# Keeping w_in's tiles as high and low parts between three passes of PackIn

## The chip, the core and the metric

The kernel runs on one core of a Trainium2 chip. The metric is the device time of one execution in microseconds (us). The engines are named as the profile does: PE (TensorE; PEld is its weight load), DVE (VectorE), ACT (ScalarE), POOL (GpSimd) and SP (SyncE, which here only issues DMA transfers).

## What is computed

Attention in two steps over 32 packed rows, then two feed-forward blocks, all in float32:

```
p_packed = softmax(p k^T / 8) v            8 batches, 8 heads, 32 x 576 x 64
x = softmax(q p_packed^T / 8) p_packed     as 4608 x 512
h = x @ w_in                               512 x 2048
x = (h * sigmoid(h)) @ w_out               2048 x 512
out = (((x @ w1) * (x @ w2)) @ w3) @ wo2
```

## The kernel before

**High and low parts.** A float32 product is made of three matmuls in the type fp32r: `mm3` (lines 97 to 100) multiplies high by high, low by high and high by low part. A part pair is made by `split_hi` (L82, a cast, on ACT as an activation or on DVE as L86) and `split_lo` (L91, a subtraction, on DVE or on POOL).

**The first half of the program** (to about 860 us) is a list of 256 items `(b, f, m)`: batch, half of its 576 rows, block of 128 of the 2048 hidden columns. For an item, `emit_h` makes ps_h (six matmuls), `emit_g` the activation: sg on ACT (L841), gg on DVE (L846), its high part gh on ACT and its low part gl on POOL; `emit_x2` multiplies by w_out three items later (`LAG = 3`) into four PSUM banks ps_x. At the end of each half the banks are emptied into xs, two of them by DVE (L883). ps_h has two buffers, so it waits for the gg of two items before.

**Where h's left factor comes from.** Attention output is never formed for the product with w_in: `PackIn` multiplies the packed rows by w_in instead (m = p_packed w_in, for two batches at once) and stores m in the DRAM tensors m_d; `fetch` loads blocks of it (tile mr), splits them (mq: high part on DVE, low part on POOL) and uses them as weights of ps_h. `Pack` and `Spread` are the two attention steps; their work (sbd, mbd, x, s, e, pk) runs mostly on DVE and ACT.

**PackIn** runs three times, for batches 2 and 3, 4 and 5, 6 and 7; its due times (`pack_in`) are items 44 to 66, 102 to 126 and 166 to 190. Each pass goes through the 16 tiles of w_in (128 x 512). The source tiles lie in the DRAM tensor wi_d, stored at the program's start. `load_w` loads one into wz (tag z, NZ = 6 buffers), and splits it into the pair wi (WI = 3 buffers): the high part on ACT (128 x 512), the low part on POOL. `steps` loads three tiles ahead; then for each tile:

```
ps = bank("ps_m")
mm3(ps[0:64 * n], m3[0], m3[1], w[:, 0], w[:, 1], True, True)
self.load_w(i + WI)
ms = at.tile([128, 512], F32, tag="ms", name="ms", bufs=NM)
split_hi(ms[0:64 * n], ps[0:64 * n], False)
```

and two `move`s store ms, whose tag has NM = 2 buffers, to m_d. The tag wi also holds raw (source words of w_in and w_out at the start) and sums (of `decode_late`).

**What sets the order.** Three streams are advanced by due times (`due`): x (attention), y (PackIn) and z (`decode_late`, late weights). `move` issues on SP's queue. `store` puts a transfer off: `flush`, called once per item, issues it on ACT's queue, with age 1 at the second flush. The framework then places each instruction by its own model of time, and keeps one in-order queue for each engine. All 16 DMA engines serve SP's queue and ACT's.

Of the kernel before, what the change touches and what calls it, by code (L numbers as in the profile page):

```python
# [9 lines left out]
F32 = mybir.dt.float32  # L10
F32R = mybir.dt.float32r
# [12 lines left out]
def attention_swiglu_chain(  # L24
# [36 lines left out]
    CD = DM // 128  # L61
# [15 lines left out]
    NSLOT, LAG, WI, KQ, NZ, NM = 8, 3, 3, 2, 6, 2  # L77
# [3 lines left out]
    def act_copy(dst, src, mul=1.0):  # L81
        return A.activation(out=dst, in_=src, func=ACTF.Copy, scale=mul)  # L82

    def split_hi(hi, src, on_vector=False):
        if on_vector:
            V.tensor_copy(out=hi, in_=src)  # L86
        else:
            act_copy(hi, src)

    def split_lo(lo, src, hi, eng=None):  # L90
        (eng or V).tensor_tensor(out=lo, in0=src, in1=hi.bitcast(F32), op=ALU.subtract)  # L91
# [5 lines left out]
    def mm3(dst, wh, wl, xh, xl, start, stop):  # L97
        T.matmul(out=dst, lhsT=wh, rhs=xh, start=start, stop=False)  # L98
        T.matmul(out=dst, lhsT=wl, rhs=xh, start=False, stop=False)  # L99
        return T.matmul(out=dst, lhsT=wh, rhs=xl, start=False, stop=stop)  # L100
# [10 lines left out]
    def move(out, in_, eng=DMA):  # L111

        out, in_ = (x.bitcast(F32) if x.dtype == F32R else x for x in (out, in_))
        with tc.issue_after(behind[eng]) if eng in behind else ExitStack():
            return eng.dma_start(out=out, in_=in_)
# [3 lines left out]
    def store(out, in_, age=1):  # L119

        stores.append([age, out, in_])
# [14 lines left out]
    dram = ctx.enter_context(tc.tile_pool(name="dram", bufs=1, space=bass.MemoryType.DRAM))  # L136
    const = ctx.enter_context(tc.tile_pool(name="const", bufs=1))
    ident = const.tile([128, 128], F32, name="ident")

    wi_d = dram.tile([4, DM, 512], F32, name="wi_d")  # L140
    w12_d = dram.tile([128, KM2 // 2, 2, 7, 2, 2, 128], F32, name="w12_d")
    w34_d = [dram.tile([128, 512], F32, name=f"w34_d{i}") for i in range(KM2)]
    late_d = {n: dram.tile([128, 512], F32, name=f"late_d{n}") for n in range(KM2, MID)}
# [5 lines left out]
    at = attn.enter_context(tc.tile_pool(name="at", bufs=1, side="right"))  # L149
# [13 lines left out]
    def bank(name):  # L163
        return ps_f.tile([128, 512], F32, tag="f", name=name)


    class Decode:
# [7 lines left out]
        def __init__(self, raw, z, ps=None):  # L175
            def word(dtype, t):
                return raw.bitcast(dtype).rearrange("p (n t) -> p n t", t=2)[:, :, t]

            high = word(F32, 1) if ps is None else ps
            act_copy(high, word(F32, 1), 2.0**-112)  # L180
            act_copy(word(I32, 0), word(U32, 0), 2.0**-29)
            high = high.bitcast(I32)
            V.tensor_scalar(out=z, in0=high, scalar1=3, scalar2=None, op0=ALU.logical_shift_left)

            V.scalar_tensor_tensor(
                out=word(I32, 0), in0=high, scalar=-(2**31), in1=word(I32, 0),
                op0=ALU.bitwise_and, op1=ALU.bitwise_or,
            )
            G.tensor_tensor(out=z, in0=z, in1=word(I32, 0), op=ALU.add)
            self.z = z.bitcast(F32)  # L190
# [41 lines left out]
    def m_blocks(plain):  # L232
        return blocks("mbd", [128, 2, CD, 2, 2, 32], plain)
# [263 lines left out]
    class PackIn:  # L497
# [2 lines left out]
        N = 17  # L500
        HOOKS = {}

        def __init__(self, bs):
            self.bs = bs
            self.w = {}

        def load(self):
# [2 lines left out]
        turn0 = turn1 = prepare = load_v = split_v0 = tail = load  # L510

        def load_w(self, i):
            if i < 4 * CD:
                g, c = divmod(i, CD)
                z = at.tile([128, 512], F32, tag="z", name="wz", bufs=NZ)
                move(out=z, in_=wi_d[g, 128 * c:128 * c + 128])
                t = at.tile([128, 2, 512], F32R, tag="wi", name="wi", bufs=WI)
                split_hi(t[:, 0], z)
                split_lo(t[:, 1], z, t[:, 0], G)
                self.w[i] = t  # L520

        def steps(self):
            n = len(self.bs)
            for i in range(WI):
                self.load_w(i)
            yield
            mbd_use[0] = self
            for i in range(4 * CD):
                g, c = divmod(i, CD)
                w = self.w.pop(i)  # L530
                ps = bank("ps_m")
                m3 = [m_blocks(False)[:, x, c, 0:n].rearrange("p b h n -> p (b h n)") for x in range(2)]
                mm3(ps[0:64 * n], m3[0], m3[1], w[:, 0], w[:, 1], True, True)
                self.load_w(i + WI)
                ms = at.tile([128, 512], F32, tag="ms", name="ms", bufs=NM)
                split_hi(ms[0:64 * n], ps[0:64 * n], False)
                for y, b in enumerate(self.bs):
                    move(
                        out=m_d[b, g][2 * c:2 * c + 2].rearrange("h n f -> (h n) f"),
                        in_=ms[64 * y:64 * y + 64],  # L540
                    )
                    if c == CD - 1:
                        m_done.add((b, g))
                if i == 4 * CD - 1:
                    mbd_use[0] = None
                yield
# [537 lines left out]
    ins = []  # L1084
# [4 lines left out]
        paces["x"].append((lo, hi, sum(u.N for u in us)))  # L1089

    def pack_in(lo, hi, bs):
        ins.append(PackIn(bs))
        paces["y"].append((lo, hi, PackIn.N))

    over(5, 14, plain([Spread(1, 0), Spread(1, 1)]))
    over(26, 38, [Pack(2, 0, 0), Pack(2, 1, 0), Pack(3, 0, 1), Pack(3, 1, 1)])
    pack_in(44, 66, [2, 3])
    over(44, 62, [Spread(2, 0), Spread(2, 1)])
    for b in range(2, B - 2, 2):
        n, at0 = b + 2, b * H2  # L1100
        over(at0 + 8, at0 + 29, [
            Pack(n, 0, 0), Pack(n, 1, 0), Spread(b + 1, 0), Spread(b + 1, 1), Pack(n + 1, 0, 1), Pack(n + 1, 1, 1)
        ])
        pack_in(at0 + 38, at0 + 62, [n, n + 1])
        over(at0 + 38, at0 + 61, [Spread(n, 0), Spread(n, 1)])
# [485 lines left out]
```

## Time and profile before

| | us |
|---|---|
| median of 3 runs (1418.19 to 1420.69) | 1419.5 |
| the profiled execution | 1418.07 |
| its span, first to last instruction | 1416.3 |

| engine | busy, share of the span |
|---|---|
| PE | 96% |
| PEld | 93% |
| DVE | 71% |
| POOL | 64% |
| ACT | 52% |

A row of the timeline gives start and duration, and in brackets how long its engine was idle just before it and what ended that. A row of windows gives each engine's busy time in a stretch, the number of its instructions, TensorE's granted clock as a share of full speed, the mean busy share of the DMA engines and their rate. Matmuls are pipelined: one of 288 columns is shown with some 0.3 us and follows the one before by about 0.13. Line numbers are those of the kernel before; in the changed kernel those up to line 500 are one higher from line 141 on, those after PackIn ten higher.

### The profile page before, as it was taken

To read this page: it belongs to the slowest core of one execution; us is meant where nothing else is said; L and a number is where in the kernel's file an instruction comes from. 1 tells how busy PE (TensorE), PEld (TensorE's weight loads), DVE (VectorE), ACT (ScalarE), POOL (GpSimd) and SP (SyncE) were. 2 spreads that over 40 slices of the span, in tenths; PEclk is the share of its full clock that TensorE was granted. 3 is DMA by queue.
4 is the path that set the end of the run, shared out by engine and by line. 5 is a ranking of instruction groups with operands and counts; after the bars stand their busy time and mean duration, and the time that the engine had idled before them with its cause. 6 is when DMAs were issued, how large, how long until landed. Compare 5 with 4: busy or idle time off the path is not lost. (4 is left out here: it accounts for less than half of the span.)

```text
span 1416.3 us, 26739 instructions
## 1 busy us (share of the span) xinstructions
PE 1364.4 (96%) x9188; PEld 1315.3 (93%) x9188; DVE 1009.3 (71%) x1764; ACT 734.0 (52%) x1643; POOL 908.0 (64%) x859
## 2 busy tenths in 40 slices
PE   7699899999999999999999999899999999999997
PEld 5488799999899999999999999899999999999997
DVE  5897857668867579877769856876765766657665
ACT  5867555655566565675456644443333443334431
POOL 2778855855779766788576653755664756647543
PEclk9999999999999999999999999999999999999998
DMA  8598544744667534685458648656767577676641
GB/s 310 199 295 273 161 153 144 220 154 140 213 185 212 179 116 143 200 245 173 134 160 256 205 139 289 215 164 208 218 174 227 180 210 218 176 228 180 209 155 45
DMA packets 191414, 272.82 MB, mean 193 GB/s; under 512 B 18736, under 2 KB 112176, under 8 KB 191280
## 3 DMA queue, kind: packets, MB, share of 16 engines
q1 hardware_dynamic: 173168, 251.20, 57.5%
q10 hardware_dynamic: 18112, 19.93, 4.1%
q8 instruction: 73, 1.20, 0.4%
q14 instruction: 61, 0.50, 0.1%
HBM read 208.93 MB, written 62.13 MB: 191 GB/s over the span
## 5 line engine op out<-in xcount | busy, mean ns | idle before, releaser
L98 PE MATMUL ps_x<-gh,wo 128*128 128x288 f32 x1024 | 301.0, 297 | 4.3 <-DVE xs L883 2.4
L99 PE MATMUL ps_x<-gh,wo 128*128 128x288 f32 x1024 | 300.3, 295 | 0.0
L100 PE MATMUL ps_x<-gl,wo 128*128 128x288 f32 x1024 | 290.1, 297 | 2.0 <-POOL gl L91 1.9
L91 POOL TENSOR_TENSOR gl<-gg,gh 128x288 fp32r<-128x288 f32 x256 | 228.8, 896 | 97.9 <-ACT gh L82 80.7
L1461 DVE TENSOR_TENSOR o<-o,ps_o 128x768 f32<-128x768 f32 x143 | 135.9, 951 | 107.7 <-PE ps_o L1480 106.7
L91 POOL TENSOR_TENSOR mq<-mr,mq 128x256 fp32r<-128x256 f32 x168 | 140.1, 834 | 93.5 <-DVE mq L86 41.9
L98 PEld LDWEIGHTS ps_x<-gh,wo 128*128 128x128 f32 x1024 | 192.2, 188 | 7.6 <-DVE xs L883 3.2
L99 PEld LDWEIGHTS ps_x<-gh,wo 128*128 128x128 f32 x1024 | 192.4, 188 | 2.0 <-issue 1.2
L100 PEld LDWEIGHTS ps_x<-gl,wo 128*128 128x128 f32 x1024 | 188.2, 188 | 4.9 <-POOL gl L91 4.0
L82 ACT ACTIVATE gh<-gg 128x288 fp32r<-128x288 f32 x256 | 112.6, 442 | 149.3 <-DVE gg L846 140.1
L846 DVE SCALAR_TENSOR_TENSOR gg<-sg,ps_h 128x288 f32<-128x288 f32 x256 | 114.4, 447 | 104.3 <-ACT sg L841 64.0
L98 PE MATMUL ps_h<-a,mq 128*128 128x288 f32 x512 | 156.4, 305 | 17.5 <-DVE gg L846 13.3
L99 PE MATMUL ps_h<-a,mq 128*128 128x288 f32 x512 | 152.5, 298 | 0.0
L100 PE MATMUL ps_h<-a,mq 128*128 128x288 f32 x512 | 152.1, 297 | 0.0
L91 POOL TENSOR_TENSOR lfa<-y,lfa 128x384 fp32r<-128x384 f32 x69 | 78.6, 1139 | 105.3 <-ACT lfa L82 89.9
L841 ACT ACTIVATE sg<-ps_h 128x288 f32<-128x288 f32 x256 | 103.1, 405 | 78.5 <-PE ps_h L100 49.9
L1480 PE MATMUL ps_o<-w,lfs 128*128 128x256 f32 x828 | 119.4, 282 | 1.9 <-DVE o L1461 1.5
L98 PEld LDWEIGHTS ps_h<-a,mq 128*128 128x128 f32 x512 | 96.9, 189 | 26.0 <-DVE gg L846 19.1
L1341 PE MATMUL ps_a<-xct,ws 128*128 128x384 f32 x576 | 116.3, 335 | 0.4 <-ACT p L82 0.4
L1480 PEld LDWEIGHTS ps_o<-w,lfs 128*128 128x128 f32 x828 | 112.4, 189 | 2.7 <-DVE o L1461 1.8
L1341 PEld LDWEIGHTS ps_a<-xct,ws 128*128 128x128 f32 x576 | 100.1, 188 | 0.7 <-ACT p L82 0.7
L99 PEld LDWEIGHTS ps_h<-a,mq 128*128 128x128 f32 x512 | 97.0, 189 | 2.7 <-issue 1.0
(202 smaller groups left out, 3299.1 us busy)
## 6 DMA issues: line engine op xcount, KB each, us to landing
ws<-w_d SPq DMA_DIRECT2D x192, 256.0 KB, 3.0
wa<-w_d SPq DMA_DIRECT2D x144, 256.0 KB, 3.1
mr<-m_d SPq DMA_DIRECT2D x144, 128.0 KB, 2.6
raw<-in_moe_w_dram SPq DMA_DIRECT2D x32, 512.0 KB, 4.5
w_d<-w12s ACTq DMA_DIRECT2D x56, 256.0 KB, 2.8
wz<-wi_d SPq DMA_DIRECT2D x48, 256.0 KB, 3.9
m_d<-ms SPq DMA_DIRECT2D x96, 128.0 KB, 3.0
x_d<-xs SPq DMA_DIRECT2D x20, 576.0 KB, 3.5
```

The lines of the kernel that those rows point to most:

```text
L82: return A.activation(out=dst, in_=src, func=ACTF.Copy, scale=mul)
L91: (eng or V).tensor_tensor(out=lo, in0=src, in1=hi.bitcast(F32), op=ALU.subtract)
L98: T.matmul(out=dst, lhsT=wh, rhs=xh, start=start, stop=False)
L99: T.matmul(out=dst, lhsT=wl, rhs=xh, start=False, stop=False)
L100: return T.matmul(out=dst, lhsT=wh, rhs=xl, start=False, stop=stop)
L841: ins = A.activation(out=sg, in_=ps, func=ACTF.Tanh, scale=0.5)
L846: ins = V.scalar_tensor_tensor(out=gg, in0=sg, scalar=1.0, in1=ps, op0=ALU.add, op1=ALU.mult)
L1341: ins = T.matmul(out=bank, lhsT=w[:, kt, wp], rhs=xt[:, kt, xp], start=first and (kt, n) == (0, 0), stop=last and (kt, n) == (1, 2), skip_ ...
L1461: V.tensor_tensor(out=oacc[k], in0=oacc[k], in1=ps, op=ALU.add)
L1480: T.matmul(out=ps[:, t], lhsT=l[:, lp], rhs=w[:, wp], start=fresh and t != 1 and n == 0, stop=done and t != 0 and n == 2, skip_group_check ...
```

## The change

In its first pass, PackIn splits each tile as before and also stores the pair, high and low part side by side (128 x 2 x 512), in one of 16 new DRAM tensors wp_d, by `store` with age 1. The second and third pass (`kept`) load the pair into the wi tile in place of wz, and split nothing. They load two tiles ahead instead of three, and issue the load of tile i + 2 ahead of tile i's matmuls.

```diff
+    wp_d = [dram.tile([128, 2, 512], F32, name=f"wp_d{i}") for i in range(4 * CD)]
...
-        def __init__(self, bs):
-            self.bs = bs
+        def __init__(self, bs, kept):
+            self.bs, self.kept = bs, kept
             self.w = {}
...
         def load_w(self, i):
-            if i < 4 * CD:
+            if i >= 4 * CD:
+                return
+            t = at.tile([128, 2, 512], F32R, tag="wi", name="wi", bufs=WI)
+            self.w[i] = t
+            if self.kept:
+                move(out=t, in_=wp_d[i])
+            else:
                 g, c = divmod(i, CD)
                 z = at.tile([128, 512], F32, tag="z", name="wz", bufs=NZ)
                 move(out=z, in_=wi_d[g, 128 * c:128 * c + 128])
-                t = at.tile([128, 2, 512], F32R, tag="wi", name="wi", bufs=WI)
                 split_hi(t[:, 0], z)
                 split_lo(t[:, 1], z, t[:, 0], G)
-                self.w[i] = t
+                store(out=wp_d[i], in_=t, age=1)
...
             n = len(self.bs)
-            for i in range(WI):
+            ahead = WI - self.kept
+            for i in range(ahead):
                 self.load_w(i)
             yield
             mbd_use[0] = self
             for i in range(4 * CD):
                 g, c = divmod(i, CD)
+                if self.kept:
+                    self.load_w(i + ahead)
                 w = self.w.pop(i)
                 ps = bank("ps_m")
                 m3 = [m_blocks(False)[:, x, c, 0:n].rearrange("p b h n -> p (b h n)") for x in range(2)]
                 mm3(ps[0:64 * n], m3[0], m3[1], w[:, 0], w[:, 1], True, True)
-                self.load_w(i + WI)
+                if not self.kept:
+                    self.load_w(i + ahead)
...
-        ins.append(PackIn(bs))
+        ins.append(PackIn(bs, bool(ins)))
```

So 32 casts on ACT and 32 subtractions on POOL go, 32 loads of 256 KB become loads of 512 KB, and 16 stores of 512 KB come in. The scheduler also places other instructions anew: the queues differ in order from about 165 us to 453 us and, on PE, from 586 to 609, and are the same elsewhere.

DVE's queue ahead of the second pass, at about 374 us (xs empties PSUM banks at the end of a half, sbd and mbd are blocks of Pack's results, mq is the high part of fetch). Before:

```order
L86 CAST mq<-mr 128x2x128
L883 TENSOR_SCALAR xs<-ps_x_4488 128x288
L253 TENSOR_TENSOR sbd_2304<-pkT,sbd_2304 32x2x32
L91 TENSOR_TENSOR w12s<-sums,w12s 128x2x128
L253 TENSOR_TENSOR sbd_2304<-pkT,sbd_2304 32x2x32 x3
L883 TENSOR_SCALAR xs<-ps_x_4490 128x288
L490 CAST mbd<-ps_pk 64x2x32
```

and with the change:

```order
L86 CAST mq<-mr 128x2x128
L893 TENSOR_SCALAR xs<-ps_x_4520 128x288
L893 TENSOR_SCALAR xs<-ps_x_4522 128x288
L470 STREAM_TRANSPOSE pkT<-pk 128x64
L856 SCALAR_TENSOR_TENSOR gg<-sg,ps_h 128x288
L86 CAST mq<-mr 128x2x128
L252 CAST sbd_2320<-pkT 32x2x32 x4
L91 TENSOR_TENSOR w12s<-sums,w12s 128x2x128
L254 TENSOR_TENSOR sbd_2320<-pkT,sbd_2320 32x2x32 x3
L491 CAST mbd<-ps_pk 64x2x32
```

The second copy of xs has moved ahead of the work on sbd, right behind the first.

ACT's queue at the start of the first pass (wi<-wz is the high part of tiles 3, 4 and 5, wp_d_65 and wp_d_66 are the stores of tiles 3 and 4, a is a part of Spread's result). Before:

```order
L82 ACTIVATE wi<-wz 128x512
L82 ACTIVATE ms<-ps_m 128x512
L841 ACTIVATE sg<-ps_h 128x288
L579 ACTIVATE s_2747<-s_2747 128x576
L82 ACTIVATE wi<-wz 128x512
L82 ACTIVATE ms<-ps_m 128x512
L82 ACTIVATE gh<-gg 128x288
L841 ACTIVATE sg<-ps_h 128x288
L82 ACTIVATE wi<-wz 128x512
```

and with the change:

```order
L82 ACTIVATE wi<-wz 128x512
L82 ACTIVATE ms<-ps_m 128x512
L851 ACTIVATE sg<-ps_h 128x288
L115 DMA wp_d_65<-wi 128x1024
L589 ACTIVATE s_2763<-s_2763 128x576
L82 ACTIVATE wi<-wz 128x512
L82 ACTIVATE ms<-ps_m 128x512
L82 ACTIVATE gh<-gg 128x288
L851 ACTIVATE sg<-ps_h 128x288
L82 ACTIVATE wi<-wz 128x512
L115 DMA wp_d_66<-wi 128x1024
```

A store stands on ACT's queue three to five instructions behind its tile's cast, and waits there for POOL's low part.

SP's queue in the second pass, with the change (wp_d_65 to wp_d_67 are tiles 3 to 5, the m_d stores those of tiles 0 and 1):

```order
L115 DMA wi<-wp_d_65 128x1024
L115 DMA m_d_0_127<-ms 64x512
L115 DMA m_d_0_131<-ms 64x512
L115 DMA kq<-in_k_dram 128x2x288 x2
L115 DMA wi<-wp_d_66 128x1024
L115 DMA m_d_0_127<-ms 64x512
L115 DMA m_d_0_131<-ms 64x512
L115 DMA wi<-wp_d_67 128x1024
```

Before, the loads of wz stood there without waiting for a matmul, in groups of up to four further ahead; now each load stands in front of the m_d stores of the tile whose buffer it takes.

## Rows read from the trace of the kernel before

**Rows 1.** The page, busy time of each engine, share of the span and instructions

```profile
PE 1364.4 (96%) x9188; PEld 1315.3 (93%) x9188; DVE 1009.3 (71%) x1764; ACT 734.0 (52%) x1643; POOL 908.0 (64%) x859
```

**Rows 2.** Windows (us; busy by engine and instructions, clock, DMA share, GB/s)

```profile
236.00:285.00 49.00, 49.00 (x333) 46.40 (x332) 32.74 (x58) 31.02 (x67) 38.08 (x39) 1.00 0.73 209
285.00:340.00 55.00, 55.00 (x420) 54.59 (x419) 36.62 (x93) 31.66 (x79) 33.63 (x38) 1.00 0.46 143
405.00:455.00 50.00, 48.76 (x331) 46.01 (x330) 38.71 (x56) 34.40 (x76) 41.30 (x39) 1.00 0.76 220
600.00:655.00 55.00, 54.72 (x378) 52.48 (x377) 40.64 (x62) 36.68 (x82) 48.67 (x46) 1.00 0.74 222
```

**Rows 3.** Waits of PE from 230 to 900 us: total, times, longest

```profile
PE ps_h L98 <- DVE gg L846: 4.1, 7, 1.1
PE ps_x L98 <- DVE xs L883: 2.2, 1, 2.2
```

**Rows 4.** Timeline of PE (start, duration, operation, idle time before and its end)

```profile
376.63 0.29 PE L99 MATMUL ps_x<-gh,wo 128*128 128x288 f32 x1
379.10 0.40 PE L98 MATMUL ps_x<-gh,wo 128*128 128x288 f32 x1 [2.19 <-DVE xs L883]
```

**Rows 5.** Timeline of DVE at the same place

```profile
375.93 2.63 DVE L253 TENSOR_TENSOR sbd<-pkT,sbd 32x64 fp32r<-32x64 f32 x3
378.59 0.46 DVE L883 TENSOR_SCALAR xs<-ps_x 128x288 f32<-128x288 f32 x1
```

**Rows 6.** Tile sbd, line 253, duration in ns as min/median/max

```profile
L253 DVE TENSOR_TENSOR sbd<-pkT,sbd x48: 205/220/1907, 170.0 to 594.9; 32x64 fp32r<-32x64 f32 x48
```

**Rows 7.** Timeline of POOL at the same place

```profile
377.22 3.72 POOL L91 TENSOR_TENSOR wi<-wz,wi 128x512 fp32r<-128x512 f32 x3
```

**Rows 8.** Windows of five microseconds behind the wait of rows 4

```profile
380.00:385.00 5.00, 5.00 (x26) 4.59 (x25) 3.66 (x11) 3.05 (x7) 3.93 (x5) 0.66 0.98 285
385.00:390.00 5.00, 5.00 (x41) 5.00 (x40) 4.42 (x12) 4.04 (x11) 2.55 (x4) 1.00 1.03 360
```

**Rows 9.** Timelines of DVE, POOL and PE ahead of pass 3

```profile
552.34 0.74 DVE L91 TENSOR_TENSOR x<-kq,x 128x576 fp32r<-128x576 f32 x1
...
581.30 3.04 DVE L91 TENSOR_TENSOR x<-kq,x 128x576 fp32r<-128x576 f32 x2
...
581.91 1.81 POOL L91 TENSOR_TENSOR wi<-wz,wi 128x512 fp32r<-128x512 f32 x1
...
585.64 0.40 PE L98 MATMUL ps_h<-a,mq 128*128 128x288 f32 x1 [0.58 <-DVE gg L846]
```

**Rows 10.** The low parts of all 48 wi tiles (us in total, mean ns)

```profile
L91 POOL TENSOR_TENSOR wi<-wz,wi 128x512 fp32r<-128x512 f32 x48 | 67.0, 1403 | 9.9 <-ACT wi L82 9.9
```

**Rows 11.** DMA, 236 to 285 us: sum, and issues with size and median landing

```profile
DMA packets 8154, 10.22 MB, mean 209 GB/s; under 512 B 880, under 2 KB 4976, under 8 KB 8150
...
m_d<-ms SPq DMA_DIRECT2D x32, 128.0 KB, 2.7
```

**Rows 12.** Groups of pass 1, the ms copies: busy, mean, idle time before

```profile
L82 ACT ACTIVATE ms<-ps_m 128x512 f32<-128x512 f32 x16 | 9.4, 586 | 2.8 <-DMA m_d<-ms 2.8
```

**Rows 13.** Timelines of ACT and POOL at the start of pass 1

```profile
239.54 0.40 ACT L841 ACTIVATE sg<-ps_h 128x288 f32<-128x288 f32 x1
...
239.23 1.36 POOL L91 TENSOR_TENSOR wi<-wz,wi 128x512 fp32r<-128x512 f32 x1 [1.55 <-ACT wi L82]
```

**Rows 14.** Timeline of ACT in pass 2

```profile
418.63 0.58 ACT L82 ACTIVATE ms<-ps_m 128x512 f32<-128x512 f32 x1
...
426.33 0.60 ACT L82 ACTIVATE ms<-ps_m 128x512 f32<-128x512 f32 x1 [0.82 <-DMA m_d<-ms]
```

**Rows 15.** Landing of the transfers of tile raw, then of ms (to m_d)

```profile
DMA to landing us min/median/max: 3.4/4.6/8.8
...
DMA to landing us min/median/max: 2.2/3.2/6.6
```

**Rows 16.** Timeline of PE behind the first splits of wi

```profile
170.17 0.40 PE L98 MATMUL ps_h<-a,mq 128*128 128x288 f32 x1 [2.38 <-DVE gg L846]
```

## The prediction

> **What bounds the kernel now.** I read the busy times of the page first. TensorE (PE) is busy for 1364.4 of 1416.3 us, VectorE (DVE) for 71% and GpSimd (POOL) for 64% [rows 1]. Work taken from ScalarE (ACT) or POOL is therefore worth only what it takes out of TensorE's idle time. The windows come next, one for each pass of PackIn: 236 to 285 us (pass 1), 405 to 455 (pass 2) and 600 to 655 (pass 3). TensorE idles 0, 1.24 and 0.28 us in them, while the DMA engines are busy for 73 to 76% [rows 2]. So the passes that lose their splits have about 1.5 us to give, and the pass that gains stores starts from none. What else there is lies ahead of passes 2 and 3, where their first three tiles are split: the table of waits names one of 2.2 us for DVE's xs and seven for DVE's gg, 4.1 us together [rows 3].
>
> I price three things: the waits beside the removed splits, the new traffic, and the new order of instructions.
>
> **A, the wait ahead of pass 2: 4.0 us gained.** TensorE issues a matmul at 376.63 and the next at 379.10, after 2.19 us of waiting for the second xs copy (L883), which empties a PSUM bank [rows 4]. On DVE that copy starts at 378.59, behind three sbd subtractions that took 2.63 us [rows 5]; the median of one is 0.22 us, the longest 1.907 [rows 6]. POOL ran the low parts of three wi tiles back to back from 377.22 for 3.72 us [rows 7], so I take the subtractions to be slowed by POOL. In the next five microseconds the granted clock is 0.66 (part of them at 1.2 GHz, after TensorE's idle time) and 26 matmuls are issued, where the five after have 41 at 1.00 [rows 8]: (41 - 26) / 41 x 5.0 = 1.8 us. The change acts twice: the three POOL operations are gone, and in DVE's new order the second xs copy stands directly behind the first, ahead of the sbd work. So I count the whole 2.2 + 1.8. The bounds are 0 (TensorE waits as long for a gg behind the moved sbd work) and 4.0.
>
> **B, inside pass 2: 0.6 gained.** TensorE's idle time there is 1.24 us [rows 2]. Thirteen of the pass's 16 ACT casts and POOL subtractions stand in this stretch, but DVE's work and the stores of m_d stay. I take half, between 0 and 1.24.
>
> **C, ahead of pass 3: 0.6 gained.** TensorE waits 0.58 us at 585.64 for a gg, which stands on DVE behind two subtractions of x that took 3.04 us; elsewhere one takes 0.74. POOL's wi subtraction ran beside them from 581.91 for 1.81 us [rows 9]. The excess of 3.04 - 1.48 = 1.56 us is more than the wait, so it goes. The 0.28 us in the pass [rows 2] I leave. Bounds: 0 and 0.9.
>
> The other splits that go, of 45 us on POOL (two thirds of 67.0 [rows 10]), count nothing: TensorE does not wait beside them.
>
> **D, the 16 stores of pass 1: 2.0 lost.** Three are issued well ahead of the pass, thirteen in it, 524,288 bytes each: 6.8 MB on top of 10.22 MB [rows 11] that keep the 16 engines busy for 73% of 49 us [rows 2]. Two windows in which the engines are full, at shares of 0.98 and 1.03, move 285 and 360 GB/s [rows 8], 322 on average. At that rate 6.8 MB take 21.1 us: 0.73 x 49 + 21.1 = 56.9 us of transfers in 49, so 7.9 us too much at the upper end. The lower end is 0: kq, xs and x_d transfers can land later, as the 55 us after the pass use only 46% [rows 2]. Where it would hurt is the ms copy. It waits on ACT until the m_d stores of the tile two before have landed; such waits already add up to 2.8 us in the pass [rows 12], and none reaches TensorE [rows 2]. Sixteen copies in 49 us are one in 3 us, so a store has some 5 us, and its median is 2.7 [rows 11]. The nearest row is thus that of the covered waits, closer to 0 than to 7.9: I take 2.0. Each store also holds ACT's queue until POOL has written the low part, and behind it stand sg, gh and the next ms copy, for which DVE and TensorE wait. For tile 3 the low part ends now at 239.23 + 1.36 = 240.59, and the sg ahead of its store at 239.54 + 0.40 = 239.94 [rows 13]: 0.65 us of waiting, on an engine that is idle for 49 - 31 = 18 us of the pass [rows 2]. It adds nothing to the 2.0.
>
> The Trainium skill, page DMA: Bandwidth & Descriptors, section Bandwidth, puts the limit of HBM per core at about 358 GB/s. By that figure pass 1 needs 17.0 MB / 358 = 47.6 of its 49 us, D is 0, and the time 1416.3. The trace agrees that such rates occur, with its one window at 360 GB/s [rows 8].
>
> **E, the loads of passes 2 and 3: 0.5 lost.** A tile now comes as 512 KB instead of 256, on SP's queue, and waits there for its buffer until the matmuls of the tile three before are done; behind it in the queue stand the m_d stores of that earlier tile, which wait for the same matmuls anyway. From there to its own matmuls there are some 7.7 us (the ms copies at 418.63 and 426.33, three tiles apart [rows 14]). Loads of 512 KB land in 4.6 us by the median, in 8.8 at most [rows 15]: normally hidden with 3 us to spare, at worst 1.1 us late. Five such late tiles would make 5.5, the upper end; the lower is 0. The added 4.2 MB per pass are 13 us at 322 GB/s and bring the share to about 1.0, hence not quite 0.
>
> **F, the new order: 1.5 lost.** What is issued between 165 and about 453 us, and between 586 and 609, comes in a somewhat other order, since the framework's scheduler places it anew. Most of that stretch now runs without a TensorE wait, so a new order can mostly add one; the present ones for gg are 4.1 / 7 = 0.6 us on average [rows 3], and I take two or three. Against that, the wait of 2.38 us at 170.17 [rows 16], beside the first stores, may shrink. I take +1.5, from -2.4 to +4.
>
> **The sum.** -4.0 - 0.6 - 0.6 + 2.0 + 0.5 + 1.5 = -1.2 us. The profiled execution took 1418.07 us; 1416.9 follows, and as it stands 1.4 below the median of 1419.5, the forecast is **1418.3**. About 0.2%, 2.8 us, is what a measurement tells from no change.
>
> **Rivals.**
> 1. The new traffic and order stay hidden (D, E and F are 0): -5.2, which gives 1414.3. For it: no wait for a store reaches TensorE in pass 1. Against: 73% of busy time before the stores. Chance 0.30. The limit of 358 GB/s on the skill's DMA page would have D that way.
> 2. The transfers of pass 1 overflow, and the kernel gets slower. Decisive is whether an m_d store lands later than some 5 us after its issue: then each ms copy holds ACT, the sg behind it comes late, then gg, and TensorE's ps_h waits. D costs 7.9: -5.2 + 7.9 + 0.5 + 1.5 = +4.7, or 1424.2. For it: a store of 512 KB is twice any transfer that a tile makes now, and one m_d store already took 6.6 us [rows 15]. Against: much of the traffic can wait. Chance 0.20.
> 3. The change does not do what it says: the waits came from DVE's own order and load, and return before another instruction. The gains are 0 and the costs hidden: 1419.5. For it: of the 4.1 us of waits for gg only 0.58 stand beside a wi split [rows 3, 9]. Chance 0.12.
>
> **The numbers.** The forecast has 0.38. Faster by over 0.2% (below 1416.7): 0.25 of rival 1 and 0.08 of the forecast's lower side, 0.33. Slower (above 1422.3): 0.17 of rival 2, 0.05 of the forecast and 0.03 of rival 3, 0.25. The rest, 0.42, lies within. The range of 1412.5 to 1425 takes in rivals 1 and 2 with 1 to 2 us to spare, and leaves out the outer ends of D, E and F, for which I keep 0.2. The forecast's own range, with D from 0 to 4 and F from -1 to 3, is 1414 to 1422.
>
> **What would show it.** Right: the wait for xs near 379 us and the low clock behind it are gone, POOL is busy for some 45 us less, the window of pass 1 shows a DMA share near 1 and waits of ms for m_d well above 2.8 us, but little idle time of TensorE. Wrong to the slow side: several microseconds of TensorE waits between 236 and 285, or waits of ps_m for the loads of wi. Wrong to the fast side: none of these, and a shorter wait near 170. Wrong in A: a new wait of the same size for gg near 380.

## The result: slower, for the greater part because a store held ScalarE's queue

| | us |
|---|---|
| forecast, with its range | 1418.3 (1412.5 to 1425.0) |
| before, median of 7 runs | 1418.86 |
| changed, median of 7 runs (1423.38 to 1431.7) | 1425.59 |
| ratio, 95% interval | 1.0054 (1.0035 to 1.0073) |
| profiled execution of the changed kernel, and its span | 1423.38, 1421.6 |

The changed kernel is slower by about half a per cent, 6.7 us by the medians: 0.6 above my range, and on the side of rival 2. The profiled execution is the fastest of the seven, so its trace shows a little less of the loss (5.3 us of span) than the median has.

**Profile after.** The busy times on the page of the profile answer to [rows 1]: POOL is busy for 41.5 us less, ACT for 14 less. The 32 splits are gone, and the kernel is slower.

```profile
PE 1362.5 (96%) x9188; PEld 1313.7 (92%) x9188; DVE 989.6 (70%) x1764; ACT 719.8 (51%) x1611; POOL 866.5 (61%) x827
```

The windows of [rows 2], in the changed kernel:

```profile
236.00:285.00 49.00, 44.71 (x296) 42.48 (x296) 30.26 (x51) 26.71 (x58) 31.05 (x31) 0.97 0.88 297
285.00:340.00 55.00, 53.53 (x398) 52.45 (x397) 32.36 (x80) 33.05 (x81) 36.28 (x41) 1.00 0.62 190
405.00:455.00 50.00, 47.27 (x322) 44.62 (x320) 31.95 (x66) 26.61 (x59) 25.21 (x28) 1.00 0.89 296
600.00:655.00 55.00, 53.04 (x367) 50.86 (x366) 33.92 (x62) 28.70 (x64) 26.55 (x30) 1.00 0.88 293
```

TensorE idles 4.29 us in pass 1 (0 before), 1.47 in the stretch behind it (0), 2.73 in pass 2 (1.24) and 1.96 in pass 3 (0.28). In all three passes the DMA engines are now busy for 88 to 89%, at some 295 GB/s. The table of TensorE's waits from 230 to 900 us answers to [rows 3] and names the two new ones:

```profile
PE ps_h L98 <- DVE gg L856: 5.0, 9, 1.1
PE ps_h L98 <- ACT a L82: 4.1, 1, 4.1
PE ps_m L98 <- DMA wi<-wp_d: 3.8, 3, 2.0
```

**The wait in pass 1** is a single one. The timeline of PE, and then that of ACT, in the changed kernel (ACTq is ACT's queue issuing a transfer):

```profile
267.89 0.29 PE L98 MATMUL ps_h<-a,mq 128*128 128x288 f32 x1
272.27 0.40 PE L98 MATMUL ps_h<-a,mq 128*128 128x288 f32 x1 [4.08 <-ACT a L82]
```

```profile
266.16 0.39 ACT L851 ACTIVATE sg<-ps_h 128x288 f32<-128x288 f32 x1
271.16 0.33 ACTq L115 DMA_DIRECT2D wp_d<-wi  x1
271.53 0.68 ACT L82 ACTIVATE a<-sT 128x576 fp32r<-128x576 f32 x1 [4.98 <-DMA kq<-in_k_dram]
```

ACT does nothing from 266.55 to 271.16. At the head of its queue stands the store of tile 10, behind it a, which TensorE needs. The trace puts the end of the wait down to the landing of a load of kq, a transfer of SP's that has nothing to do with w_in. The program's order, with what each instruction waits for, tells why:

```
L115 DMA wp_d10_72<-wi_3236 128x1024 [waits DMAHW4_49,Pool_49]
```

The store waits for POOL's low part, and for one of eight semaphores that all transfers of SP's and ACT's queues take in turn: it may go only when the transfer that used the same one last has landed. Here that is the second of two loads of kq, which SP issues from 261.13 to 262.41, the second for 0.59 us, so from 261.82 on (timeline of SP). The view of tile kq from 255 to 265 us gives the landing of the two loads, first in the kernel before, then now:

```profile
261.13 1.28 SPq L115 DMA_DIRECT2D kq<-in_k_dram  x2
```

```profile
DMA to landing us min/median/max: 5.6/6.0/6.4
...
DMA to landing us min/median/max: 8.7/9.0/9.3
```

261.82 + 9.3 is 271.1, when the store goes out. Behind the wait TensorE's clock falls, as the windows of the changed kernel show:

```profile
268.00:273.00 5.00, 0.92 (x7) 0.73 (x6) 0.75 (x2) 1.47 (x4) 0.62 (x2) 0.99 0.99 360
273.00:278.00 5.00, 5.00 (x28) 5.00 (x27) 2.61 (x7) 2.64 (x7) 4.18 (x5) 0.66 0.94 311
```

A clock of 0.66 over five microseconds (part of them at 1.2 GHz in place of 2.4) costs (1 - 0.66) x 5 = 1.7 us. So pass 1 loses 4.1 + 1.7 us in one place.

**The waits in passes 2 and 3** are three late loads, in the timeline of PE:

```profile
421.22 0.47 PE L98 MATMUL ps_m<-wi,mbd 128*128 128x512 f32 x1 [0.58 <-DMA wi<-wp_d]
443.44 0.48 PE L98 MATMUL ps_m<-wi,mbd 128*128 128x512 f32 x1 [1.24 <-DMA wi<-wp_d]
615.88 0.47 PE L98 MATMUL ps_m<-wi,mbd 128*128 128x512 f32 x1 [1.96 <-DMA wi<-wp_d]
```

SP issued them at these times (timeline of SP), and the pair loads from 405 to 455 us landed as the third line says (view of tile wp_d):

```profile
414.99 0.94 SPq L115 DMA_DIRECT2D wi<-wp_d  x1
437.14 0.62 SPq L115 DMA_DIRECT2D wi<-wp_d  x1
...
608.05 0.55 SPq L115 DMA_DIRECT2D wi<-wp_d  x1
```

```profile
DMA to landing us min/median/max: 4.4/5.9/7.5
```

From issue to the moment at which TensorE could have used the tile there were 5.1 to 5.9 us (421.22 - 0.58 - 414.99 = 5.65 for the first).

**What was won** is there as well: no wait for the second xs copy near 379 us, and the clock behind it is full, where [rows 8] had 0.66.

```profile
380.00:385.00 5.00, 5.00 (x40) 4.95 (x38) 4.58 (x14) 1.74 (x6) 2.77 (x4) 1.00 0.58 199
```

### The profile page after: what moved, and what is told of

Same layout as the page of the kernel before. It is cut to its first block, busy times and chain, and to the rows that moved or that the text cites. A ratio compares the mean times of both kernels' runs of the same rounds, so it can differ in the third digit from the quotient of the medians.

```text
span 1421.6 us, 26734 instructions
## 1 busy us (share of the span) xinstructions
PE 1362.5 (96%) x9188; PEld 1313.7 (92%) x9188; DVE 989.6 (70%) x1764; ACT 719.8 (51%) x1611; POOL 866.5 (61%) x827
```

## The experiments

Theories: H, a store that waits at the head of ACT's queue holds the work behind it; T, the bytes fill the DMA engines and make everything late on any queue; O, the new order of instructions costs; L or E, the larger loads of passes 2 and 3 cost. The diffs are against the changed kernel unless another is named; every ratio is against the kernel before, run beside it on the same chip.

| kernel | median us | before | ratio (95%) |
|---|---|---|---|
| e1_stores_only | 1427.64 | 1419.06 | 1.0069 (1.0052 to 1.0087) |
| e2_loads_only | 1420.68 | 1419.06 | 1.0010 (0.9999 to 1.0022) |
| e3_small_stores | 1419.07 | 1419.06 | 1.0002 (0.9992 to 1.0013) |
| e5_pool_stores | 1428.81 | 1419.06 | 1.0080 (1.0063 to 1.0096) |
| e6_keep3 | 1414.41 | 1418.94 | 0.9969 (0.9958 to 0.9980) |
| e7_pool_late | 1424.06 | 1418.94 | 1.0036 (1.0023 to 1.0049) |
| e9_half_loads | 1415.51 | 1418.94 | 0.9978 (0.9968 to 0.9988) |
| e10_keep6 | 1417.69 | 1418.94 | 0.9989 (0.9979 to 0.9999) |
| e11_stores_gap | 1428.20 | 1418.69 | 1.0069 (1.0056 to 1.0081) |
| e4_sp_stores | 1421.64 | 1418.69 | 1.0027 (1.0016 to 1.0039) |
| e12_keep3_sp | 1414.97 | 1418.48 | 0.9977 (0.9967 to 0.9987) |
| e13_stores_only_sp | 1421.14 | 1418.48 | 1.0015 (1.0004 to 1.0026) |

### Stores alone, and stores of a sixteenth

```diff
-                store(out=wp_d[i], in_=t, age=1)
+                if len(ins) == 1 or self is ins[0]:
+                    store(out=wp_d[i], in_=t, age=1)
...
-        ins.append(PackIn(bs, bool(ins)))
+        ins.append(PackIn(bs, False))
```

> The first pass stores its 16 pairs as in the changed kernel, passes 2 and 3 split every tile as before, and nothing reads the stored pairs. Up to about 380 us it has the changed kernel's instructions in the changed kernel's order. Theory H (a store waits at the head of ACT's in-order queue for an earlier transfer of SP's to land, and holds a, gh and sg behind it): the trace of the changed kernel has 4.1 us of TensorE waiting for a near 272 us, 1.5 us more idle time from 285 to 340 and a granted clock of 0.97 over 49 us (1.5 us), 7.1 us together, and none of it depends on the later loads; so 1418.9 + 7.1 = 1426.0, with the wait for a of about 4 us near 270. Theory L (the loss is made by the 512 KB loads of passes 2 and 3): 1418.9 within 2 us. Theory O (the loss is the new order): as H, so this run does not tell H from O.

Measured: 8.6 us slower, with the wait where it was expected (timeline of PE, windows):

```profile
275.81 0.61 PE L98 MATMUL ps_h<-a,mq 128*128 128x288 f32 x1 [4.53 <-ACT a L82]
```

```profile
273.00:278.00 5.00, 2.19 (x9) 2.19 (x10) 1.57 (x2) 2.02 (x4) 1.83 (x2) 0.57 0.87 315
278.00:283.00 5.00, 5.00 (x29) 4.87 (x28) 2.47 (x6) 2.08 (x5) 2.79 (x4) 0.75 0.93 293
```

The loss is made by the stores, not by what reads them. The next kernel stores 8 partitions of the 128; the diff is against e1_stores_only (both conditions let the first pass alone store):

```diff
-                if len(ins) == 1 or self is ins[0]:
-                    store(out=wp_d[i], in_=t, age=1)
+                if self is ins[0]:
+                    store(out=wp_d[i][0:8], in_=t[0:8], age=1)
```

> As e1_stores_only, but each store moves 8 of the 128 partitions, 32 KB in place of 512, and nothing reads them: the same 16 issues at nearly the same places of ACT's queue, a sixteenth of the bytes. Theory H with the traffic as its cause (a store waits long only because the transfers ahead of it land late when the DMA engines are full): landings return to some 3 us, no store holds ACT for more than 1 us, and the time is 1418.9 within 2 us. Rival I (the issue itself, or its wait for POOL's low part, is what costs): 1426, as e1_stores_only. Rival O (the new order between 165 and 453 us): also 1424 to 1426, since that order differs from the one of the kernel before in the same way.

Measured: no difference from the kernel before. So the 16 issues on ACT cost nothing by themselves, and rival I is out. O is out only in part: the queues of this kernel differ from those of the kernel before from 158 to 292 us and have the old order again behind that, not the changed kernel's order up to 453 us that the expectation counted on. What the new order costs behind 292 us this run does not test. H and T are not told apart yet, since both need the bytes.

### The same bytes on another queue

```diff
-                store(out=wp_d[i], in_=t, age=1)
+                move(out=wp_d[i], in_=t, eng=G)
```

> The changed kernel, with each of the 16 stores issued on POOL's queue right behind the low part that POOL writes, in place of ACT's queue one item later. The bytes are the same. Theory H: ACT no longer waits for a store, so the 4.1 us for a and the low clock behind it (1.5) are gone: 1425.6 - 5.6 = 1420.0, with a DMA share in the first pass still near 0.9. Theory T (the full DMA engines make mr, kq, wz and the m_d stores late, whichever engine issues the stores): as the changed kernel, 1425.6 within 2 us, with TensorE's waits in the first pass at other instructions but of the same sum, 4 us or more. What speaks for a slower result: POOL spends time on each issue and its mq and gl come later.

Measured: 3.2 us slower than the changed kernel by the medians. That is on the slow side, as T or the price of POOL's issues would have it, but the place is neither's: from 230 to 300 us TensorE waits 2.1 us, none for a, and the clock from 268 to 283 stays at 1.00. What is lost lies at 171 us, ahead of the pass (timelines of PE and DVE, then windows):

```profile
171.48 0.61 PE L98 MATMUL ps_h<-a,mq 128*128 128x288 f32 x1 [5.70 <-DVE gg L856]
```

```profile
162.86 7.88 DVE L252 CAST sbd<-pkT 32x64 fp32r<-32x64 f32 x4
```

```profile
170.00:175.00 5.00, 2.10 (x7) 1.79 (x8) 4.71 (x12) 1.15 (x3) 2.73 (x4) 0.50 0.26 105
175.00:180.00 5.00, 5.00 (x23) 5.00 (x23) 4.34 (x10) 2.60 (x6) 2.19 (x2) 0.54 0.10 26
```

Four casts to sbd took 7.88 us beside POOL's work, and the gg that TensorE waits for stands behind them. So the run did not decide; the next one moves only the stores from the fourth on.

```diff
-                store(out=wp_d[i], in_=t, age=1)
+                if i < WI:
+                    store(out=wp_d[i], in_=t, age=1)
+                else:
+                    move(out=wp_d[i], in_=t, eng=G)
```

> The changed kernel, its first three stores on ACT's queue as they are, the other thirteen on POOL's, each right behind the low part. It takes e5_pool_stores apart, which lost 3.6 us more by a wait of 5.70 and by a low clock of 10.24 us near 170, and won the wait for a and the low clock behind it near 272. Theory H (ACT's in-order queue held by a store is the loss of the first pass): no wait for a near 270 and no low clock there; TensorE's idle time from 236 to 292 falls from 4.3 to about 2.2 us: 1425.6 - 2.1 - 1.7 = 1421.8. Theory T (the full engines make others late by as much): 1425.6 within 1.5. Theory P (POOL's time for issuing costs more than ACT's hold): over 1427.

Measured: 1424.06, 1.5 under the changed kernel, where H had 3.8 and T at most 1.5; by the time alone it lies at the edge of T, and the intervals of the two ratios overlap, so the time does not decide. The trace agrees with H in the place: the wait is 1.49 us, for gg, and the clock behind it 1.00.

```profile
270.43 0.40 PE L98 MATMUL ps_h<-a,mq 128*128 128x288 f32 x1 [1.49 <-DVE gg L859]
```

SP's queue holds nothing but transfers, so a store that waits there holds no arithmetic:

```diff
-    def store(out, in_, age=1):
+    def store(out, in_, age=1, eng=A):
...
-        stores.append([age, out, in_])
+        stores.append([age, out, in_, eng])
...
-                move(x[1], x[2], A)
+                move(x[1], x[2], x[3])
...
-                store(out=wp_d[i], in_=t, age=1)
+                store(out=wp_d[i], in_=t, age=1, eng=DMA)
```

> The changed kernel with all 16 stores issued on SP's queue, at the same age, in place of ACT's. Bytes and number are the same. Theory H (what costs in the first pass is that ACT's queue, with a, sg and gh in it, is held): SP holds only transfers, so no wait for a near 270, and at least what e7_pool_late gained over the changed kernel: 1424 or less, down to 1421.8 if nothing else comes late. Theory Q (any in-order queue that is held costs as much, since the m_d stores, wz, mr and kq stand behind the store on SP): 1425.6 or more, with waits of ms for m_d, or of mq for mr, in place of the wait for a.

Measured: 1421.64, 4.0 under the changed kernel, as H has it. The window of pass 1, and the group of ms copies from 236 to 292:

```profile
236.00:285.00 49.00, 48.21 (x332) 46.08 (x331) 31.12 (x51) 28.77 (x60) 35.19 (x34) 1.00 0.90 307
```

```profile
L82 ACT ACTIVATE ms<-ps_m 128x512 f32<-128x512 f32 x16 | 9.5, 593 | 11.4 <-DMA m_d<-ms 11.4
```

The engines are as full as in the changed kernel (0.90, 307 GB/s). The ms copies wait 11.4 us for m_d stores, four times the 2.8 of [rows 12], and TensorE idles 0.79 us in place of 4.29. The same move without the later loads makes the price of the bytes plain; the diff against e1_stores_only is that of e4_sp_stores:

> As e1_stores_only, which was 8.6 us slower than the kernel before: passes 2 and 3 split as before, nothing reads the 16 stored pairs, and the stores are issued on SP's queue in place of ACT's. Theory H (the bytes cost little, ACT's held queue does): no wait for a near 270, and 1427.6 - 4.5 (that wait) - 3.4 (the half clock behind it) = 1419.7. Theory T (the bytes cost, on any queue): 1427.6 within 2. Half and half, as e4_sp_stores against the changed kernel (4.0 less): 1423.6.

Measured: 2.7 us slower than the kernel before, 5.9 less than the same stores on ACT's queue (each against the kernel before beside it). T's 1427.6 is out; H's 1419.7 is the nearest, 1.4 away, half and half 2.5. With the queue, other things change too: the order on DVE, ACT and PE from about 160 to 330 us, and the landing of the kq loads (5.6 us by the median in e4_sp_stores, 255 to 270 us, where the changed kernel had 9.0). So these two runs price the queue as a whole; that the hold is the largest part of it is read from the traces. In pass 1 of e13_stores_only_sp TensorE idles 1.0 us, at the ms copies, as these waits from 230 to 300 us show:

```profile
PE ps_m L98 <- ACT ms L82: 1.0, 2, 0.5
```

Most of what is left is lost behind the pass. The two windows of e13_stores_only_sp, and the second one of e3_small_stores:

```profile
236.00:285.00 49.00, 48.00 (x331) 45.75 (x329) 33.59 (x59) 28.74 (x61) 32.59 (x32) 1.00 0.85 287
285.00:340.00 55.00, 53.16 (x394) 51.82 (x393) 33.42 (x81) 33.03 (x82) 38.25 (x42) 1.00 0.59 188
...
285.00:340.00 55.00, 55.00 (x421) 54.83 (x421) 37.47 (x96) 31.93 (x80) 34.56 (x39) 1.00 0.47 149
```

In the pass 331 matmuls are issued, nearly the 333 of [rows 2]; in the 55 us behind it 394 where [rows 2] has 420, with 1.84 us of idle time, for gl and gg. The changed kernel has 398 there, e1_stores_only 395, e4_sp_stores 400, e3_small_stores 421. All kernels with the full stores lose some 3 us in that stretch, on either queue (26 of 420 matmuls in 55 us are 3.4). The trace of e13_stores_only_sp is the slowest of its twelve executions, but that of e4_sp_stores, among its fastest, shows the same. Whether transfers that land late do it or the new order, which e3_small_stores does not have there, no run separates: that stays open.

The Trainium skill, page DMA: Bandwidth & Descriptors, section Rules for kernel authors, says that spreading transfers over the issuing engines brings no bandwidth, since all run on the same 16 DMA engines, and only saves issue time. The rates agree (297 GB/s with the stores on ACT, 307 on SP). What the choice of queue is worth here, 4 to 6 us, is another thing, by the traces mainly what stands behind the transfer that waits.

### One hold taken away

Against e1_stores_only:

```diff
-                if len(ins) == 1 or self is ins[0]:
+                if self is ins[0] and i not in (9, 10, 11):
```

> As e1_stores_only, without the stores of tiles 9, 10 and 11 (nothing reads them): 13 stores in place of 16. In e1_stores_only the store of tile 10 stood at the head of ACT's queue until 274.7 us, when a load of kq landed that had been issued 9.4 us before; a, gh and sg stood behind it, and TensorE waited 4.5 us, with a granted clock of one half in the 6.8 us from 273.7 on. Theory H (that one hold is most of the 8.6 us by which e1_stores_only is slower than the kernel before): the hold and the low clock are gone, 1427.6 - 4.5 - 3.4 = 1419.7. Theory T (every store costs its share by filling the DMA engines): 1427.6 - 8.6 x 3 / 16 = 1426.0.

Measured: 1428.20, both wrong. The hold is gone as H had it: no wait of TensorE from 180 to 300 us. Inside the pass that can be priced, with the windows of e1_stores_only and then of this run:

```profile
236.00:292.00 56.00, 51.47 (x340) 49.21 (x339) 32.25 (x57) 29.21 (x62) 35.42 (x35) 0.94 0.82 275
...
236.00:292.00 56.00, 56.00 (x387) 53.53 (x386) 33.53 (x66) 32.25 (x70) 37.39 (x38) 1.00 0.84 281
```

At about the same share of the DMA engines (0.82 and 0.84) 47 matmuls more are issued, some 6.8 us' worth at this run's rate, and the kernel before has 386 in this stretch. But the scheduler, with three stores fewer, placed DVE's work anew, and a wait of 3.64 us with half clock behind it stands at 307.80 (timelines of PE and DVE):

```profile
307.80 0.61 PE L98 MATMUL ps_h<-a,mq 128*128 128x288 f32 x1 [3.64 <-DVE gg L857]
```

```profile
304.31 2.67 DVE L91 TENSOR_TENSOR x<-kq,x 128x576 fp32r<-128x576 f32 x2
```

Two x subtractions, which take 0.74 us each elsewhere [rows 9], stand in front of the gg; before them DVE had itself waited 2.09 us for a load of mr:

```profile
301.81 0.29 DVE L86 CAST mq<-mr 128x256 fp32r<-128x256 f32 x1 [2.09 <-DMA mr<-m_d]
```

So a late transfer and the new order meet there, and which of them costs how much was not separated. The total time of this run therefore does not price the hold (its trace is also the slowest of its six executions, 1432.45); the windows of the pass do.

### Loads alone, and loads of half the bytes

```diff
-                move(out=t, in_=wp_d[i])
+                move(out=t, in_=wp_d[0])
...
-                store(out=wp_d[i], in_=t, age=1)
+                if i == 0:
+                    store(out=wp_d[i], in_=t, age=1)
```

> Only the first tile's pair is stored, at about 157 us; passes 2 and 3 load that one pair 16 times each in place of the right ones, so the values are not those of the reference, while the loads have the changed kernel's number, size and queue. The first pass has no store. Theory H: the 7.1 us of the first pass are gone; what is left against the kernel before is the idle time of passes 2 and 3 in the changed kernel (1.5 and 1.7 us more) less the wait and the low clock near 380 (2.2 + 1.8) and some 0.5 ahead of pass 3: -1.3, so 1417.6. Theory L: 1418.9 + 7 = 1426. Theory O (new order from 165 us on): the order up to 380 us is here that of the kernel before, so the same 1417.6 as H.

Measured: 1420.68, 3.1 above the expectation of H and O. L's 1426 is out, but the loads cost more than I read from the changed kernel: five waits of ps_m for them, 4.7 us, and half clock behind the one of 2.05 us at 419.96. Against it, half of each load:

```diff
-                move(out=t, in_=wp_d[0])
+                move(out=t[:, 0], in_=wp_d[0][:, 0])
...
-                mm3(ps[0:64 * n], m3[0], m3[1], w[:, 0], w[:, 1], True, True)
+                mm3(ps[0:64 * n], m3[0], m3[1], w[:, 0], w[:, 1 - self.kept], True, True)
```

> As e2_loads_only, but passes 2 and 3 load only the high half of the one stored pair, 256 KB in place of 512, and use it for the low part as well, so the values are not those of the reference; number, kind and order of the matmuls stay. Theory E (the 512 KB loads land late because passes 2 and 3 have no room on the DMA engines for 4.2 MB more): the bytes are those of the kernel before, the loads land in 3 to 4 us, no wait of ps_m for wi is left, and the time is 1420.7 - 4.7 (these waits) - 1.7 (the low clock near 421) = 1414.3. Rival B (they are late because a load waits for its buffer, two tiles ahead in place of three, whatever its size): the waits of ps_m for wi stay above 3 us in all, and the time is 1419.5 or more.

Measured: 1415.51, 5.2 under e2_loads_only; no wait for wi is left, and passes 2 and 3 are nearly free of idle time:

```profile
405.00:455.00 50.00, 50.00 (x347) 48.12 (x346) 30.72 (x61) 29.65 (x65) 28.71 (x32) 1.00 0.86 269
600.00:655.00 55.00, 54.95 (x383) 52.93 (x382) 30.06 (x63) 30.96 (x69) 32.43 (x37) 1.00 0.81 250
```

The loads wait for their buffers as before, two tiles ahead, so it is the bytes (E), not the buffer (B). The loads landed in 4.3 us by the median in pass 2 (405 to 455 us), where the 512 KB loads of e2_loads_only took 6.6. On PE the order of the matmuls differs from that of e2_loads_only in some places from 412 us on, so the 5.2 is the price of the bytes with that difference in it.

### Fewer tiles

```diff
-            if self.kept:
+            if self.kept and i < WI:
...
-            ahead = WI - self.kept
+            ahead = WI
...
-                if self.kept:
-                    self.load_w(i + ahead)
...
-                if not self.kept:
-                    self.load_w(i + ahead)
+                self.load_w(i + ahead)
...
-                store(out=wp_d[i], in_=t, age=1)
+                if self is ins[0] and i < WI:
+                    store(out=wp_d[i], in_=t, age=1)
```

> Only the first three tiles, which are split ahead of the pass at 153 to 162 us, are stored (three stores, of 512 KB each) and loaded as pairs in passes 2 and 3; the other thirteen are split in each pass as before, three tiles ahead. Theory H (stores cost where they meet full DMA engines, which is at 250 to 272 us): these three meet a share of 0.45 and cost nothing; near 380 POOL no longer runs three low parts back to back. DVE's queue has there the order of the kernel before, with the three sbd subtractions ahead of the second xs copy, so this run shows whether POOL's work alone made them slow: if so, the wait of 2.2 us and the low clock behind it (1.7) are gone, and 0.6 ahead of pass 3: 1418.9 - 4.5 = 1414.4. Rival S (it is DVE's order, or other POOL work, that makes the second copy late): the wait stays at 2 us or more, and the time is 1418.9 within 1.5.

Measured: 1414.41, 4.5 faster than the kernel before and 11 faster than the changed one: the version that beats both. The mechanism is half of what I expected. DVE's timeline, where [rows 5] had 2.63 us, and the wait that was 2.2 us in [rows 3]:

```profile
375.30 1.66 DVE L254 TENSOR_TENSOR sbd<-pkT,sbd 32x64 fp32r<-32x64 f32 x3
```

```profile
PE ps_x L98 <- DVE xs L891: 1.2, 1, 1.2
```

Without the three low parts the subtractions are quicker, but still slow beside POOL's mq and gl; the wait is 1.2 us, and now the clock behind it stays full. So 1.0 us of the wait went, with the low clock and the wait of 0.6 ahead of pass 3: some 3.3 of the 4.5 us. The idle time inside the passes is as before, and where the rest was won was not found; that the median meets its expectation to a hundredth is luck. The Trainium skill, page SBUF — State Buffer, section Who interferes with whom, says that a VectorE instruction with two SBUF inputs contends with a GpSimd instruction that reads SBUF. These subtractions have two, and the trace agrees: 0.55 us each here against a median of 0.22 [rows 6].

Six tiles in place of three (6 for WI in the two conditions):

> As e6_keep3, with the first six tiles: three stores more, at 238 to 246 us, at the start of the first pass. In the trace of the changed kernel the transfers issued there landed in 3.3 to 5.8 us, and the backlog that held ACT grew only from 250 on, with the ninth of its stores and the transfers of x_d, xs and kq. Theory H: no store holds ACT for long, so the same 1414.4 as e6_keep3 or up to 0.5 less, for three splits fewer in each of passes 2 and 3. Rival N (each store in the pass costs its share of the 7 us, 0.5 us): 1414.4 + 1.5 = 1416.

Measured: 1417.69, slower than three tiles by 3.3 us and than either expectation. No store held ACT for long (one wait for a, 0.33 us). The trace shows small waits that e6_keep3 lacks: 0.4 us of ps_m for a pair, 0.6 of ps_w, 0.9 of ps_e behind 860 us. They don't make up 3.3. The two traces are already 1.9 us apart at 236 us, where their programs have not differed yet, so part of the difference between these two traces lies in the executions; that of the medians stays open.

The three stores of e6_keep3 on SP's queue, with the lines on eng of e4_sp_stores:

> As e6_keep3, its three stores on SP's queue in place of ACT's. The queues of DVE and TensorE then keep the order of the kernel before up to 190 us, and e4_sp_stores, which has the same start, waited 1.21 + 1.46 us near 170 with a full clock behind it, where e6_keep3 waited 3.49 with 3.4 us of half clock behind it. If that is the work of the store's place on ACT's queue (theory H, of the early stores too): 1414.4 - 0.8 - 1.7 = 1411.9. If the early waits only vary (rival V: the wait near 170 is there in every kernel, 3.5 to 3.7 us in sum, whatever the queue): 1414.4 within 1.0.

Measured: 1414.97, the time of rival V, but not by its condition: the waits near 170 were 1.21 and 1.47 us, 2.7 together as the other side had it, and the median did not move. For these early stores the queue makes no difference.

## Why the prediction was wrong, term by term

| term | predicted | measured | by |
|---|---|---|---|
| A + B + C, waits beside the splits | -5.2 | -3.4 | e9_half_loads |
| D, stores of pass 1 (with the order that they bring) | +2.0 | +8.6 on ACT, +2.7 on SP | e1, e13 |
| E, loads of passes 2 and 3 | +0.5 | +5.2 | e2 less e9 |
| F, new order | +1.5 | not measured; 0.0 where it ends at 292 us | e3_small_stores |

**A, B and C were right in kind.** In e9_half_loads the low clock near 380, the idle time of pass 2 and the wait at 585 are gone, and the xs wait is 1.2 us in place of 2.2: DVE keeps its old order there, with the sbd work ahead of the copy, and A is smaller by that.

**D failed, at a named sentence**: that a store "holds ACT's queue until POOL has written the low part", 0.65 us at a place with idle time, and "adds nothing to the 2.0". I priced one of the two semaphores that the store waits for and overlooked the other, an earlier transfer of SP's. When landings grow from 6 to 9 us, that one holds ACT for 4.6, and TensorE loses 4.1 us and 1.7 of clock. The path that I did price, ms copies waiting for m_d, costs little: on SP's queue, where it is what remains in the pass, ms waits of 11.4 us (e4_sp_stores) leave TensorE idle for 0.8 us, in e13_stores_only_sp for 1.0. That the 2.7 us of e13_stores_only_sp lie near my 2.0 is luck: by the traces most of them are lost from 285 to 340 us, the stretch that I took to be free because it uses 46% of the engines. Rival 2 had the full engines and the slow side right, and its 1424.2 is near 1425.59, but by that same covered path, so that is luck as well; it was not ms that held ACT.

**E failed by size.** I took a landing of 4.6 us and 7.7 us of room. With the engines busy for 0.89 of the pass the landing is 5.9 by the median and up to 7.5, and the late loads had 5.1 to 5.9 us, since SP issues a load only after what stands ahead of it.

**F was not measured.** e3_small_stores, without loss, has a new order only up to 292 us. (The two kernels' queues also differ a little further than was said ahead of the prediction: on DVE in places from 577 to 624 us, on PE to 630.)

**The limit of 358 GB/s**, from the Trainium skill's page DMA: Bandwidth & Descriptors, section Bandwidth, would have made D zero. Pass 1 did move its bytes at up to 360 GB/s for five microseconds; and here the measurement decides: in e4_sp_stores the window from 273 to 278 us moved 382 GB/s, more than that limit. In the changed kernel a transfer landed after 9 us at such a rate, and it is the landing that the store, and behind it TensorE, waited for.

The measured terms don't add up on ACT's queue: e1_stores_only and e2_loads_only lose 8.6 + 1.6 = 10.2 us, both together 6.7. On SP's they do within the intervals: 2.7 + 1.6 = 4.3 against 2.95. One reason can be read at A. The changed kernel's order up to 380 us with the splits kept (e1_stores_only) has no wait for xs near 379, but one for gg with a low clock behind it, which the prediction named as the sign of being wrong in A (timeline of PE, then window):

```profile
390.04 0.61 PE L98 MATMUL ps_h<-a,mq 128*128 128x288 f32 x1 [2.27 <-DVE gg L857]
```

```profile
390.00:395.00 5.00, 4.96 (x27) 4.96 (x28) 3.94 (x13) 3.22 (x8) 4.68 (x6) 0.69 1.04 370
```

With the splits gone and the old order (e9_half_loads, e6_keep3) the clock is full, but a wait of 1.2 us for xs stays. Only both together, in the changed kernel, remove the whole. How much of the 3.5 us that explains was not measured.

## What to carry to other kernels

Before a transfer is put on a compute engine's queue, list every semaphore that it waits for, those of earlier transfers too: all that stands behind it on that engine waits for the slowest of them. Where the DMA engines are at three quarters already, price added traffic by the longer landing of the transfers that others wait for, not by the sum of the bytes. Of a change that moves work into memory, try the part that falls into a quiet stretch by itself: three tiles of 16 brought 4.5 us, all 16 lost 6.7.

## What I had not expected of the chip

TensorE's clock does not follow a wait in the same way each time. A wait of 3.47 us near 170 has a full clock behind it in the changed kernel, and half clock for part of the next five microseconds in e7_pool_late, which has the same wait:

```profile
170.00:175.00 5.00, 4.95 (x37) 4.75 (x37) 4.66 (x12) 4.11 (x11) 4.19 (x5) 1.00 0.25 83
```

```profile
170.00:175.00 5.00, 4.75 (x24) 4.58 (x25) 3.87 (x14) 3.32 (x8) 2.30 (x3) 0.67 0.26 105
```

That is 37 matmuls against 24 in the same time, some 1.7 us. Differences of a microsecond or two between single traces are therefore no evidence without the medians; why the trace of the changed kernel is faster than its median may be this, but was not tested.
